# Ranks in place of due times: a new order of operations for an attention and feed-forward kernel on one core

## The chip, the cores and the metric

The kernel runs on one core of a Trainium2 chip. A core has a matrix engine (TensorE, PE in the profile; its weight loads are listed as PEld), three engines for elementwise work (VectorE or DVE, ScalarE or ACT, GpSimd or POOL) and a queue that issues DMAs (SyncE or SP). Each engine runs its own list of instructions in order and waits for the others through semaphores. SBUF is the on-chip memory, PSUM the smaller one that TensorE writes its sums to. The metric is the time of one execution on the device in microseconds (us).

## What is computed

Attention with random features, and then a feed-forward network with GELU. Shapes: batch 8, 8 heads, 576 positions, head dimension 64, 128 features; 4608 tokens of width 512, inner width 2048; everything in fp32.

```python
def phi(x):
    proj = np.einsum('bhsd,md->bhsm', x, omega)
    sq = np.sum(x * x, axis=-1, keepdims=True) / 2.0
    h = proj - sq
    h = h - np.max(h, axis=-1, keepdims=True)
    return np.exp(h) / np.sqrt(m)
q_p, k_p = (phi(q_s), phi(k_s))          # q_s, k_s: q and k times D**-0.25
kv = np.einsum('bhsm,bhsd->bhmd', k_p, v)
z = np.sum(k_p, axis=2)
num = np.einsum('bhsm,bhmd->bhsd', q_p, kv)
den = np.einsum('bhsm,bhm->bhs', q_p, z)[..., None] + 1e-06
x = num / den                            # tokens x 512
h = x @ w_in
g = 0.5 * h * (1.0 + erf(h / sqrt(2)))
out = g @ w_out
```

The term `sq` is the same for all features of a position, so it cancels in `h - max(h)`; the kernel leaves it out.

## The kernel before

**Units and blocks.** The attention is cut into 32 units: unit `u` is one batch and a pair of heads (`u.b`, `u.j`, number `u.k`). The feed-forward part is cut into 18 blocks of 256 tokens. A block can start once the units that hold its tokens are done, so units and blocks are woven into each other: block 0 after the four units of batch 0, then as many units as the next block needs, then that block, and so on.

**Plain and split units.** Units 0 to 7 are "plain" (`unit_plain`): fp32 matmuls throughout. `pair` and `shared` project q and k onto the features into PSUM, `top` takes the negative maximum per row on DVE, the exponential goes to the SBUF buffer `et`, `kv` (18 matmuls, line 797) sums over the positions, `q_trans` and `q_copy` transpose the q part, `num_plain` multiplies, and `den`, `rcp` and `div` normalise. Units 8 to 31 are "split" (`split_pre`, `exps_op`, `split_post`): the operands are cut into a high and a low half (`x_high`, `x_low`, `k_high`, `k_low`, `q_high`, `q_low`, `v_a`, `v_b`) so that the matmuls run on fp16.

A plain unit takes its exponential in one of two ways, by `u.mode`. In mode 0 (units 0 to 3) ACT reads each 128 x 128 tile from PSUM, with the negative maximum as the bias: `exp_tiles`, line 781, 18 instructions a unit in five groups of 4, 4, 2, 4 and 4 tiles. In mode 1 (units 4 to 7) DVE first subtracts the maximum while it copies a group from PSUM to `et` (`shift_tiles`, line 786, five instructions a unit), and then one instruction takes the exponential of the whole unit in SBUF (`exps`, line 790, 128 x 2304). Split units use line 790 as well.

**Weights.** `w_in` and `w_out` come as eight pieces each of 1 MB of raw 64-bit values (`w_load`, two DMAs a piece). ACT (`w_hi`, `w_lo`), DVE (`w_shift`, `w_max`) and POOL (`w_round`) turn a piece into fp32 and find its largest value. When all pieces of a matrix are in, `wchain_a` to `wchain_f` make its scale (two small steps on PE, `wchain_b` at line 643 and `wchain_d`). Then `weights_sums` prepares `w_in` for the later blocks (`a_high`, `a_low`, `a_high2`, `a_low2`, `s_sum`, `s_high`, `s_low`) and `weights_split` cuts `w_out` into fp16 halves (`w_high`, line 602, on ACT, and `w_low`, line 605, on DVE, 16 pieces each).

**Blocks.** Block 0 uses fp32 weights (`mm1`, `gelu_plain`, `mm2_plain`). Blocks 1 to 17 use seven products of half-size matrices for the first layer, in fp16 halves: `sw1`, then `comb_a` to `comb_c` on ACT and DVE, then `sw2` (line 1279 is the matmul of both), then `gelu`, `g_high`, `g_low`, and the second layer `mm2` (lines 1327 to 1329), in 8 chunks `c`. `store` copies the sums out, `store_dma` writes them.

**The order.** No engine finds its order by itself. Each step of the work is registered with `op(engine, duration, function, ...)` with what it reads (`r`), writes (`w`) and which ring of buffers it takes a new one from (`new`; for PSUM the rings `at`, `h` and `acc`). The class `Planner` then plays the whole kernel through with these durations in `run`: at every moment each engine takes, from those operations that are ready and find a buffer, the one that is most urgent, and the operation is issued at that point of the list. `order` dependencies in `put` keep each engine to that list on the chip. What "most urgent" means is the due time: `run` works it out backwards from the start times `STARTS` and `UDUE`, adds a correction by kind of operation (`OFF`, by the name and class of unit) and one by operation (`PO`), and takes off a bonus by group (`bonus`). The durations include a price for a change of the activation table on ACT (`tsw`, 1.28 us), because exp and gelu stand in different tables.

Of the kernel before, what the change touches and what calls it, by code (L numbers as in the profile page):

```python
# [41 lines left out]
OFF = dict(a_high=-13.69, a_high2=-2.55, a_low=3.92, a_low2=30.54, back=-0.66, back_c=-53.08, block_be=18.21, block_high=2.46,  # L42
        block_high_1=-26.27, block_low=1.36, block_low_1=-19.02, block_out=1.79, block_scales=-9.32, block_spread=8.72,
        bound_a=-5.8, bound_a_a=-478.94, bound_a_b=1.62, bound_a_c=6.31, bound_b=0.18, bound_b_a=-192.28, bound_b_b=-308.58,
        bound_b_c=14.95, bound_c=-4.72, bound_c_a=85.34, bound_c_b=-108.59, bound_c_c=8.05, chain_a=-1.54, chain_b=3.92,
        chain_c=66.41, chain_d=2.96, comb_a=0.61, comb_a_1=1.25, comb_b=-1.27, comb_b_1=-14.65, comb_c=-0.14, comb_c_1=-8.99,
        den_a=-450.06, den_b=-18.7, div_a=-474.39, div_b=-35.9, exp_tiles_a=88.01, exps=3.6, exps_b=74.83, exps_c=21.55,
        g_high=-0.99, g_high_1=-58.14, g_low=-11.39, g_low_1=2.86, gelu=0.98, gelu_1=3.81, gelu_plain=-27.15, identity=-18.43,
        k_high=-2.66, k_high_c=15.22, k_low=-3.41, k_low_c=-24.51, k_shift=-2.42, k_shift_c=1.96, kv_a=-4935.28, kv_a_c=86.01,
        kv_b=-28.56, kv_b2=-1.97, kv_b2_c=14.8, kv_b_c=17.09, kv_c=7.39, kv_c_c=-27.26, kv_d=2.75, kv_d_c=12.39, kv_split=-2.52,  # L50
        kv_split_c=-3.32, kvz_plain_a=-243.1, kvz_plain_b=5.35, load_dup=-31.91, load_dup_c=179.73, load_om=15.98,
        load_two_a=-43.39, load_two_b=-51.4, load_v_a=-56.35, load_v_b=-128.76, load_vst=52.48, load_vst_c=22.44, mm1=15.82,
        mm2=25.3, mm2_1=0.3, mm2_plain=18.77, norm=-13.96, norm_c=4.14, nothing=1.34, num=-6.46, num_c=15.2, num_plain_a=-13.88,
        num_plain_b=-10.89, p2=2.99, pair_a=-272.72, pair_b=121.03, proj=0.47, proj_add=0.18, proj_add_c=-12.11, proj_c=0.24,
        proj_lo=0.22, proj_lo_c=-23.83, proj_q=0.39, proj_q_c=-12.62, put_x=-2.32, put_x_c=-12.75, q_back=2.77, q_back_c=8.16,
        q_blocks=2.07, q_blocks_c=-41.78, q_copy_a=-396.58, q_copy_b=-6.38, q_high=-0.51, q_high_c=21.5, q_low=0.22,
        q_low_c=-0.57, q_max=2.12, q_max2=0.92, q_max2_c=10.36, q_max3=13.21, q_max3_c=18.46, q_max4=-11.32, q_max4_c=7.99,
        q_max5=0.92, q_max5_c=3.49, q_max6=-15.37, q_max6_c=94.79, q_max_c=-114.63, q_shift=-18.3, q_shift_c=-152.32,
        q_trans_a=513.45, q_trans_b=-13.77, rcp_a=-364.04, rcp_b=29.11, s_high=36.92, s_low=-50.32, s_sum=-467.63,
        scale_om=-24.66, shared_a=-708.55, shared_b=-11.95, shift_tiles_b=7.13, split_om=-36.34, store=-53.19, store_dma=0.58,  # L60
        sw1=0.55, sw1_1=17.68, sw2=0.57, sw2_1=2.01, t_sum=3.22, t_sum_1=-27.4, top_a=-128.4, top_b=-0.8, v_a=4.39, v_a_c=91.42,
        v_b=0.99, v_b_c=-16.74, v_max=-14.06, v_max_c=47.43, v_scales=4.0, v_spread=32.29, vb_ones=-35.4, w_abs_1=-722.49,
        w_hi_0=1.8, w_hi_1=-202.85, w_high=-23.19, w_lo_0=3.69, w_lo_1=-90.29, w_load_0=202.81, w_load_1=4.68, w_low=-134.68,
        w_max_0=5.38, w_max_1=258.53, w_round_0=-55.99, w_round_1=-43.44, w_shift_0=8.21, w_shift_1=6.84, warm=198.7,
        wchain_a=-48.44, wchain_b=43.0, wchain_c=-25.75, wchain_d=7.44, wchain_e=16.02, wchain_f=-27.17, x_high=6.09,
        x_high_c=-14.76, x_low=-3.36, x_low_c=-0.55, zeros=37.43)
# [182 lines left out]
class Planner:  # L249
# [45 lines left out]
    def run(self, lat, hop, alloc, put):  # L295
        for o in reversed(self.ops):
            k, n, x, add = o.own or (0, 0, 0.0, 0.0)
            o.due = 1e9 if k == 0 else UDUE[n] if k == 2 else add if k == 3 else add + STARTS[n] + (STARTS[n + 1] - STARTS[n] if n + 1 < len(STARTS) else 48.0) * x
            for s in o.succ:
                o.due = min(o.due, s.due - o.c - (lat.get(o.e, 0) + hop.get(s.e, 0) if s.e != o.e else 0))  # L300
# [1218 lines left out]
```

## Time and profile before

| | |
|---|---|
| median of 3 runs | 972.83 us (969.47 to 973.82) |
| the profiled execution | 974.43 us, of which the span from its first to its last instruction is 972.4 us |
| instructions | 25715 |
| mean granted TensorE clock | 0.982 |
| data moved | 71.44 MB, mean 73 GB/s |

How to read the lines below. A line of the busy times gives an engine, its busy us, its share of the span and its instructions. A row of slices has 40 digits, each the busy tenths of 1/40 of the span (24.3 us); `PEclk` is the granted clock in the same manner. A group is `line engine operation output<-inputs (shape) xcount | busy us, mean ns of one | idle us of the engine just before them <- what ended that idle time`. A wait is `waiting engine, tile and line <- what ended it: us in total, times, longest us`. The chain of work that ended last is `start us, length us, what`; it is the path that one finds by going back from the last instruction, at each step to what released it.

### The profile page before, as it was taken

To read this page: it belongs to the slowest core of one execution; us is meant where nothing else is said; L and a number is where in the kernel's file an instruction comes from. 1 tells how busy PE (TensorE), PEld (TensorE's weight loads), DVE (VectorE), ACT (ScalarE), POOL (GpSimd) and SP (SyncE) were. 2 spreads that over 40 slices of the span, in tenths; PEclk is the share of its full clock that TensorE was granted. 3 is DMA by queue.
4 is the path that set the end of the run, shared out by engine and by line. 5 is a ranking of instruction groups with operands and counts; after the bars stand their busy time and mean duration, and the time that the engine had idled before them with its cause. 6 is when DMAs were issued, how large, how long until landed. Compare 5 with 4: busy or idle time off the path is not lost.

```text
span 972.4 us, 25715 instructions
## 1 busy us (share of the span) xinstructions
PE 934.6 (96%) x9956; PEld 692.8 (71%) x9956; DVE 762.8 (78%) x2134; ACT 736.2 (76%) x1573; POOL 485.1 (50%) x717
## 2 busy tenths in 40 slices
PE   7979997889999999899999999999999999999998
PEld 6757655567776777677787777867776777786776
DVE  3878888999987998887987899788888897753432
ACT  5968868688889878877877887888787898653432
POOL 0335663775658545754638564397546764300100
PEclk7979998999999999999999999999999999999999
DMA  8865332223221313121212131212121200000000
GB/s 227 236 187 176 131 92 89 65 85 88 61 64 50 97 43 92 44 74 53 82 40 73 53 96 53 72 40 85 51 72 51 72 26 23 2 24 12 12 23 22
DMA packets 46313, 71.44 MB, mean 73 GB/s; under 512 B 13680, under 2 KB 22256, under 8 KB 46192
## 3 DMA queue, kind: packets, MB, share of 16 engines
q1 hardware_dynamic: 46192, 69.81, 23.9%
q8 instruction: 78, 1.28, 0.5%
q14 instruction: 43, 0.35, 0.1%
HBM read 60.36 MB, written 9.44 MB: 72 GB/s over the span
## 4 chain that ended last, share of the span: by engine, by line
PE 74%; DVE 9%; ACT 5%; POOL 5%; DMA 3%; issue 3%; SPq 1%; POOLq 0%; ACTq 0%; DVEq 0%
PE h L1279 26%; PE acc L1327 9%; PE acc L1328 9%; PE acc L1329 9%; PE h L1266 3%; PE acc L1320 3%; PE at L1007 2%; PE at L1092 2%; PE at L1029 2%; PE at L852 2%; PE at L797 1%; DVE w L1082 1%; DVE gl L1317 1%; DMA vt<-in_v 1%; POOL r L999 1%
## 5 line engine op out<-in xcount | busy, mean ns | idle before, releaser
L999 POOL TENSOR_TENSOR r<-xt,r 64x288 fp32r<-64x288 f32 (+2 forms) x216 | 165.9, 784 | 144.7 <-ACT r L994 83.7
L1279 PE MATMUL h<-xh,w 128*128 128x128 f16 x2176 | 216.2, 219 | 0.0
L1328 PE MATMUL acc<-woh,gl 128*128 128x512 f16 (+1 forms) x544 | 206.0, 379 | 2.5 <-DVE gl L1317 2.5
L1327 PE MATMUL acc<-woh,gh 128*128 128x512 f16 (+1 forms) x544 | 207.0, 381 | 0.9 <-ACT o L1336 0.9
L1329 PE MATMUL acc<-wol,gh 128*128 128x512 f16 (+1 forms) x544 | 205.8, 378 | 0.2 <-DVE wol L605 0.2
L1279 PE MATMUL h<-xl,w 128*128 128x128 f16 x1088 | 198.6, 219 | 0.0
L1279 PEld LDWEIGHTS <-w 128*128 128x128 f16 x3264 | 195.4, 98 | 3.3
L1279 PE MATMUL h<-xh,wih 128*128 128x128 f16 x816 | 157.2, 220 | 8.5 <-DVE gl L1317 4.8
L1279 PE MATMUL h<-xl,wih 128*128 128x128 f16 x816 | 156.5, 219 | 0.0
L1279 PE MATMUL h<-xh,wil 128*128 128x128 f16 x816 | 156.5, 219 | 0.0
L1279 PEld LDWEIGHTS <-wih 128*128 128x128 f16 x1632 | 139.7, 98 | 18.3 <-DVE h L1297 4.1
L1317 DVE SCALAR_TENSOR_TENSOR gl<-h,bs,gh 128x512 f16<-128x512 f32 x136 | 101.0, 744 | 46.2 <-ACT gh L1314 45.7
L1305 ACT ACTIVATE h<-h,bs 128x512 f32<-128x512 f32 x136 | 90.0, 662 | 49.0 <-PE h L1279 42.7
L1314 ACT ACTIVATE gh<-h,bs 128x512 f16<-128x512 f32 x136 | 93.6, 689 | 36.0 <-PE acc L1329 28.9
L1329 PEld LDWEIGHTS <-gh 128*128 128x128 f16 x560 | 55.1, 98 | 63.5 <-issue 1.7
L1279 PEld LDWEIGHTS <-wil 128*128 128x128 f16 x816 | 80.1, 98 | 17.0 <-issue 7.9
L994 ACT CAST r<-xt 128x256 fp32r<-128x256 f32 (+2 forms) x216 | 81.7, 407 | 13.2 <-PE at L1029 7.6
L1328 PEld LDWEIGHTS <-gl 128*128 128x128 f16 x560 | 55.2, 99 | 47.0 <-DVE gl L1317 3.0
L1327 PEld LDWEIGHTS <-gh 128*128 128x128 f16 x560 | 55.0, 98 | 47.2 <-issue 2.1
L1286 ACT COPY g<-h 128x256 f32<-128x256 f32 x136 | 50.4, 370 | 40.8 <-PE h L1279 38.5
L1291 DVE TENSOR_TENSOR g<-h,g 128x128 f32<-128x128 f32 x136 | 38.5, 283 | 39.0 <-ACT g L1286 38.3
L1292 DVE TENSOR_TENSOR h<-h,g 128x256 f32<-128x256 f32 x136 | 58.8, 433 | 4.7
(231 smaller groups left out, 2106.7 us busy)
## 6 DMA issues: line engine op xcount, KB each, us to landing
xt<-in_kT SPq DMA_DIRECT2D x56, 288.0 KB, 3.9
xt<-in_qT SPq DMA_DIRECT2D x56, 288.0 KB, 3.8
out_x<-o SPq DMA_DIRECT2D x35, 256.0 KB, 2.0
raw<-in_w_in SPq DMA_DIRECT2D x16, 512.0 KB, 6.6
raw<-in_w_out SPq DMA_DIRECT2D x16, 512.0 KB, 4.6
w<-in_v SPq DMA_DIRECT2D x24, 320.0 KB, 2.9
vt<-in_v SPq DMA_DIRECT2D x8, 320.0 KB, 4.6
out_x<-o SPq DMA_DIRECT2D x2, 128.0 KB, 1.8
```

The lines of the kernel that those rows point to most:

```text
L994: nc.scalar.copy(G['r', u, x][:, 0:b - a], xf[:, a:b])
L999: nc.gpsimd.tensor_tensor(r, xf[D:, a:b], r, op=ALU.subtract)
L1279: nc.tensor.matmul(h, w[p], x[r], start=first and i + m == 0, stop=last and i == 1 and m == 2, skip_group_check=True)
L1286: nc.scalar.copy(G['sa', n, c], G['h', n, c][:, 0:2 * P])
L1291: nc.vector.tensor_tensor(q, hv[:, 3], sa[:, 0:P], op=ALU.add)
L1292: nc.vector.tensor_tensor(hv[:, 1:3], hv[:, 1:3], q.unsqueeze(1).broadcast_to([P, 2, P]), op=ALU.add)
L1305: nc.scalar.activation(h, h, AF.Gelu, scale=G['bs', n][:, 2:3])
L1314: nc.scalar.activation(G['gh', n, c], G['h', n, c], AF.Copy, scale=G['bs', n][:, 3:4])
L1317: nc.vector.scalar_tensor_tensor(G['gl', n, c], G['h', n, c], G['bs', n][:, 3:4], G['gh', n, c], op0=ALU.mult, op1=ALU.subtract)
L1327: nc.tensor.matmul(acc, gh, woh[:, f, c0:c1], start=f == 0, stop=False)
L1328: nc.tensor.matmul(acc, gl, woh[:, f, c0:c1], start=False, stop=False)
L1329: nc.tensor.matmul(acc, gh, wol[:, f, c0:c1], start=False, stop=f == NF - 1)
```

## The change

Four things change at once; what each instruction computes is the same but for the second point.

1. **Ranks.** `STARTS`, `UDUE`, `OFF`, `PO`, the bonuses and the backward pass are gone. In their place stands `RANK`, a list of 4665 numbers, one for each registered operation in the order of registration. The numbers count for each engine by itself: the 1181 operations of PE have the ranks 0 to 1180, the 1384 of ACT 0 to 1383, the 1349 of DVE, 599 of POOL and 150 of SP likewise. Of the operations that are ready, the one with the lowest rank goes first.
2. **Exponentials of units 4 to 7.** `X['tiles']=8` puts these units into mode 0, so they use `exp_tiles` instead of `shift_tiles` and `exps`. The choice of PSUM rings stays as it was (by `u.b` instead of `u.mode`).
3. **Durations.** Some 20 durations that the plan assumes are set anew, and on PE 0.057 us is added where a projection of a split unit follows other kinds of work (`psw`, `ptab`).
4. **Small things.** `store` is now entered as a user of the buffer `bs` that it reads. `put` gets code for filling idle time of PE with extra matmuls, which is multiplied by `fill=0.0` and issues nothing.

```diff
-X = dict(fb=0.0, fbp=0.0, fb0=-33.65, fbb=0.17, fbw=46.38, pm=0.15, tsw=1.28, plain=8, kvp=8, eb0=8, ttr=1,
+X = dict(pm=0.15, tsw=1.28, psw=0.057, plain=8, tiles=8, fill=0.0, kvp=8, eb0=8, ttr=1,
...
-STARTS = (116.55, 138.26, 186.0, 230.93, 278.01, 329.62, 369.41, 415.44, 460.86, 506.44, 553.03, 597.34, 643.92, 691.78, 735.98,
...
+RANK = (0, 0, 0, 0, 1, 5, 2, 3, 8, 1, 2, 49, 4, 7, 2, 3, 5, 9, 16, 17, 13, 11, 3, 17, 38, 30, 4, 11, 13, 14, 2, 12, 19, 13, 20, 23, 25, 21, 23, 36,
...
+        1151, 1154, 1155, 1150, 1153, 1369, 1337, 1338, 1159, 1371, 1372, 1341, 1158, 1161, 1163, 1156, 1157, 1370, 1339, 1340, 1160, 1373, 1374,
...
+PO = {}
...
     def run(self, lat, hop, alloc, put):
-        for o in reversed(self.ops):
-            k, n, x, add = o.own or (0, 0, 0.0, 0.0)
...
-            o.due += PO.get(o.id, 0.0)
         for o in self.ops:
-            o.due += OFF.get(o.tag, 0.0)
+            o.due = RANK[o.id]
...
-                if o.tab and o.tab != self.tab:
+                if o.e == 'PE':
+                    c += X['psw'] * (o.tab == 'r' and self.ptab is None)
+                    self.ptab = o.tab
+                elif o.tab and o.tab != self.tab:
...
-                    p = (o.due - bonus.get(o.kind, 0.0), o.id)
+                    p = o.due
...
-            op('POOL', 0.84, s_sum, c, k, ...
-        op('ACT', 0.6, a_high, c, r=[a, sc], w=[('ah', c)], kind='W')
-        op('DVE', 0.75, a_low, c, r=[a, sc, ('ah', c)], w=[('al', c)], kind='W')
-        op('ACT', 0.38, a_high2, c, r=[b, sc], w=[('ah2', c)], kind='W')
-        op('DVE', 0.42, a_low2, c, r=[b, sc, ('ah2', c)], w=[('al2', c)], kind='W')
+            op('POOL', 0.78, s_sum, c, k, ...
+        op('ACT', 0.68, a_high, c, r=[a, sc], w=[('ah', c)], kind='W')
+        op('DVE', 0.92, a_low, c, r=[a, sc, ('ah', c)], w=[('al', c)], kind='W')
+        op('ACT', 0.46, a_high2, c, r=[b, sc], w=[('ah2', c)], kind='W')
+        op('DVE', 0.47, a_low2, c, r=[b, sc, ('ah2', c)], w=[('al2', c)], kind='W')
...
-            u.mode = 0 if b == 0 else 1 if u.k < X['plain'] else 2
+            u.mode = 0 if u.k < X['tiles'] else 1 if u.k < X['plain'] else 2
...
-        ring = ANY if u.mode == 0 else 'at'
-        op('PE', 1.0, num_plain, u, half, ...
-        op('ACT', 0.5, den, u, half, r=pn, new=[('dt', ('dt', u, half))])
+        ring = ANY if u.b == 0 else 'at'
+        op('PE', 1.15, num_plain, u, half, ...
+        op('ACT', 0.35, den, u, half, r=pn, new=[('dt', ('dt', u, half))])
...
-        op('PE', 0.77, kv_split, u, ...
+        op('PE', 0.87, kv_split, u, tab='q', ...
...
-                    op('ACT', 0.68 if n else 0.6, store, n, i, c0, c1, r=[key] + ([('bo', n)] if n >= N32 else []), ...
+                    op('ACT', 0.68 if n else 0.6, store, n, i, c0, c1, r=[key] + ([('bo', n), ('bs', n)] if n >= N32 else []), ...
...
     def put(o):
         n = len(nc.cur_bb.bb.instructions)
+        if X['fill'] and o.idle > 0.9 and o.t > 5.0:
...
         o.fn(*o.a)
```

The other durations that change: `x_low` 0.26 to 0.2 us plus its part by size, `norm` 0.75 to 0.85, `num` 0.47 to 0.46, `back` and `put_x` shorter by 0.02 and 0.11, `q_back` 0.74 to 0.71, `t_sum` 0.84 to 0.79, `block_high` and `block_low` longer by some 0.06 and 0.14, `comb_a` 0.37 to 0.33, `g_high` 0.7 to 0.66.

More of the change, by code (lines that the diff above doesn't have):

```diff
@@ L42 @@
[L42 to L66, printed above, removed]
@@ L295, in run @@
     def run(self, lat, hop, alloc, put):
[L296 to L303 removed]
         for o in self.ops:
[L305 removed]
+            o.due = RANK[o.id]
             o.left, o.ready, o.end, o.out = len(o.deps) + len(o.after), 0.0, None, False
         free, cand = {e: 0.0 for e in ('PE', 'ACT', 'DVE', 'POOL', 'SP')}, {e: [] for e in ('PE', 'ACT', 'DVE', 'POOL', 'SP')}
[L308 to L309 removed]
+        self.tab, self.ptab, self.dma, now, n = None, None, 0.0, 0.0, 0
         port = {'DVE': 0.0, 'POOL': 0.0}
@@ L319, in emit @@
                 alloc(name, k)
+            o.idle = t - max(free[o.e], o.free) if o.e == 'PE' else 0.0
             put(o)
@@ L349, in room @@
         def room(o):
-            t, o.pick, taken = o.ready, [], {}
+            t, o.pick, taken, o.free = o.ready, [], {}, 0.0
             if o.e == 'POOL':
@@ L373, in room @@
                 t = max(t, best[0])
+                o.free = max(o.free, best[0])
                 o.pick.append(best[1])
@@ L455, in favor_attention_ffn @@
     wi32 = w32f[:, 1].rearrange("p c (j w) -> p c j w", j=NJ)
+    id16 = ident.bitcast(BF16)
     ones = cp.tile([1, P], F32, name="ones")
@@ L921, in out_ops @@
         pn = [('pn', u, half, a) for a in range(2)]
-        ring = ANY if u.mode == 0 else 'at'
-        op('PE', 1.0, num_plain, u, half, r=[('qh', u, g) for g in (0, 1, 2)] + [('kvz', u), ('qh', u)] + old, w=keys, new=[(ring, k) for k in pn] + new)
-        op('ACT', 0.5, den, u, half, r=pn, new=[('dt', ('dt', u, half))])
+        ring = ANY if u.b == 0 else 'at'
+        op('PE', 1.15, num_plain, u, half, r=[('qh', u, g) for g in (0, 1, 2)] + [('kvz', u), ('qh', u)] + old, w=keys, new=[(ring, k) for k in pn] + new)
+        op('ACT', 0.35, den, u, half, r=pn, new=[('dt', ('dt', u, half))])
         op('DVE', 1.13, rcp, u, half, r=[('dt', u, half)], new=[('rt', ('rt', u, half)), ('rc', ('rc', u, half))])
@@ L938, in out_split @@
             keys, new, old = places(u, ps)
-            op('PE', 0.11 * n + 0.03, back, u, g, r=[('nx', u), ('nx', u, 0), ('nx', u, 1), 'ident'], new=[(('at', 'h'), ('px', u, g))])
-            op('ACT', sum(0.17 + (c1 - c0) / 1200 for _, c0, c1, _ in ps), put_x, u, g, due=(2, 2 * u.k + g, 0.0, 0.0), r=[('px', u, g)] + old, w=keys, new=new)
+            op('PE', 0.11 * n + 0.01, back, u, g, tab='q', r=[('nx', u), ('nx', u, 0), ('nx', u, 1), 'ident'], new=[(('at', 'h'), ('px', u, g))])
+            op('ACT', sum(0.06 + (c1 - c0) / 1200 for _, c0, c1, _ in ps), put_x, u, g, due=(2, 2 * u.k + g, 0.0, 0.0), r=[('px', u, g)] + old, w=keys, new=new)
     def unit_plain(u):
@@ L1207, in split_post @@
             op('POOL' if X['klp'] else 'DVE', 0.25 + 0.3 * n if X['klp'] else 0.14 + 0.15 * n, k_low, u, g, r=es, w=[('kk', g)])
-        op('PE', 0.77, kv_split, u, r=['vb'] + [('kk', g) for g in range(len(KG))], w=[], new=[('at', pk), ('kvs', ('kvs', u)), ('kvz', ('kvz', u))])
+        op('PE', 0.87, kv_split, u, tab='q', r=['vb'] + [('kk', g) for g in range(len(KG))], w=[], new=[('at', pk), ('kvs', ('kvs', u)), ('kvz', ('kvz', u))])
         op('ACT', 0.22, kv_a, u, r=[pk], w=[('kvs', u)])
@@ L1215, in split_post @@
         for g in range(2):
-            op('DVE', 0.74, q_back, u, g, r=[('eq', u.eb, y) for y in (g, g + 2)], new=[('qt', ('qt', u, g))])
+            op('DVE', 0.71, q_back, u, g, r=[('eq', u.eb, y) for y in (g, g + 2)], new=[('qt', ('qt', u, g))])
             op('ACT', 0.62, q_high, u, g, r=[('qt', u, g)] + ([('qf', u)] if g else []), w=[('qf', u, g)], new=[] if g else [('qf', ('qf', u))])
@@ L1358, in block_prep @@
         for k in range(4):
-            op('POOL', 0.84, t_sum, n, k, r=xr + [t + (0,)] * (k == 1) + [t + (1,)] * (k == 3) + [t] * (k > 0), w=[t + (k,)], new=[] if k else [('ts', t)], kind='B')
+            op('POOL', 0.79, t_sum, n, k, r=xr + [t + (0,)] * (k == 1) + [t + (1,)] * (k == 3) + [t] * (k > 0), w=[t + (k,)], new=[] if k else [('ts', t)], kind='B')
         for p in range(4):
@@ L1362, in block_prep @@
             ts = [t] + [t + (k,) for k in range(2 * p - 4, 2 * p - 2)] if p > 1 else []
-            op('ACT', 0.16 + m / 1200, block_high, n, p, r=[('bs', n)] + (ts or xr) + xt[:1] * (p > 0), w=[('xh', n, p)], new=[] if p else [('xh', ('xh', n))], kind='B')
-            op('DVE', 0.1 + m / 940, block_low, n, p, r=[('bs', n), ('xh', n), ('xh', n, p)] + (ts or xr) + xt[1:] * (p > 0), w=[('xl', n, p)],
+            op('ACT', 0.2 + m / 1150, block_high, n, p, r=[('bs', n)] + (ts or xr) + xt[:1] * (p > 0), w=[('xh', n, p)], new=[] if p else [('xh', ('xh', n))], kind='B')
+            op('DVE', 0.24 + m / 940, block_low, n, p, r=[('bs', n), ('xh', n), ('xh', n, p)] + (ts or xr) + xt[1:] * (p > 0), w=[('xl', n, p)],
                new=[] if p else [('xl', ('xl', n))], kind='B')
@@ L1381, in ffn_first @@
                new=[] if p else [('h', hk)], due=(1, n, (c + p * .28) / NS, 0.0), kind='P')
-        op('ACT', 0.16 + 256 / 1200, comb_a, n, c, r=[hk], new=[('g', ('sa', n, c))], kind='F')
+        op('ACT', 0.33, comb_a, n, c, r=[hk], new=[('g', ('sa', n, c))], kind='F')
         op('DVE', 0.65, comb_b, n, c, r=[('sa', n, c)], w=[hk], new=[('g', ('qs', n, c))], kind='F')
@@ L1386, in ffn_first @@
         op('ACT', 0.15 + 512 / 1000, gelu, n, c, r=[('bs', n)], w=[hk], tab='g', kind='F')
-        op('ACT', 0.7, g_high, n, c, r=[('bs', n), hk], new=[('gh', ('gh', n, c))], kind='F')
+        op('ACT', 0.66, g_high, n, c, r=[('bs', n), hk], new=[('gh', ('gh', n, c))], kind='F')
         op('DVE', 0.71, g_low, n, c, r=[('bs', n), hk, ('gh', n, c)], new=[('gl', ('gl', n, c))], kind='F')
@@ L1400, in ffn_second @@
                 if c == nc_ - 1:
-                    op('ACT', 0.68 if n else 0.6, store, n, i, c0, c1, r=[key] + ([('bo', n)] if n >= N32 else []), w=[('o', n, i)] if c0 else [],
+                    op('ACT', 0.68 if n else 0.6, store, n, i, c0, c1, r=[key] + ([('bo', n), ('bs', n)] if n >= N32 else []), w=[('o', n, i)] if c0 else [],
                        new=[] if c0 else [('o', ('o', n, i))], due=(1, n + 1, (lag + i * .6) / nc_, 0.0), kind='F' if n >= N32 else 'F0')
@@ L1480, in put @@
         n = len(nc.cur_bb.bb.instructions)
+        if X['fill'] and o.idle > 0.9 and o.t > 5.0:
+            t = [G[k] for (_, k), name in zip(o.new, o.pick) if name in ANY]
+            for _ in range(int((o.idle - 0.3) * X['fill'] / 0.11) if t else 0):
+                nc.tensor.matmul(t[0][:, 0:256], id16[:, 0:P], id16, start=True, stop=True)
         o.fn(*o.a)
```

21 lines of the change are left out of this document (7 added, 14 removed), and 334 rows, old and new, of tables (PO, RANK, UDUE).

## The prediction

> **What bounds the kernel now.** The page comes first: its span, its busy times, the slices with the granted clock, the shares of the chain.
>
> ```profile
> span 972.4 us, 25715 instructions
> ...
> PE 934.6 (96%) x9956; PEld 692.8 (71%) x9956; DVE 762.8 (78%) x2134; ACT 736.2 (76%) x1573; POOL 485.1 (50%) x717
> ...
> PE   7979997889999999899999999999999999999998
> ...
> PEclk7979998999999999999999999999999999999999
> ...
> PE 74%; DVE 9%; ACT 5%; POOL 5%; DMA 3%; issue 3%; SPq 1%; POOLq 0%; ACTq 0%; DVEq 0%
> ```
>
> TensorE (PE) is busy for 934.6 of 972.4 us, and the change adds no matmul and takes none away. So a better order can win only the 37.8 us in which PE is idle, and what the lower clock costs around them: both rows of slices fall below 9 in the same places, the first, third and seventh slice. The windows by stage say how much lies where (columns: length, then busy us and instructions of PE, PEld, DVE, ACT, POOL, then granted clock, DMA share, GB/s).
>
> ```profile
> 0.00:75.00 75.00, 62.27 (x498) 48.65 (x499) 49.95 (x124) 55.84 (x130) 20.02 (x19) 0.86 0.75 221
> 75.00:150.00 75.00, 75.00 (x441) 49.54 (x439) 63.14 (x120) 59.07 (x94) 46.33 (x50) 1.00 0.38 127
> 150.00:200.00 50.00, 39.97 (x361) 26.75 (x360) 46.20 (x117) 39.12 (x83) 29.68 (x55) 0.93 0.21 64
> 200.00:500.00 300.00, 291.00 (x3360) 219.67 (x3360) 261.20 (x779) 246.99 (x543) 179.59 (x267) 0.99 0.24 69
> 500.00:850.00 350.00, 347.12 (x3968) 259.27 (x3967) 295.46 (x894) 285.77 (x640) 203.91 (x321) 1.00 0.19 55
> 850.00:972.00 122.00, 119.22 (x1338) 88.90 (x1335) 46.84 (x102) 49.40 (x87) 5.60 (x8) 1.00 0.05 19
> ```
>
> PE idles for 12.7 us in the first 75, not at all in the next 75, then for 10.0 us in the 50 in which the weights of the second layer are split, 9.0 us in 200 to 500, 2.9 us in 500 to 850 and 2.8 us at the end. Three fifths of the idle time lies in the first fifth of the span. The list of PE's waits says what ends it (us in total, times, longest), and the chain shows the longest single obstacle and what a pause does to the clock.
>
> ```profile
> PE at L797 <- ACT et L790: 5.4, 1, 5.4
> PE at L797 <- DMA vt<-in_v: 4.9, 1, 4.9
> PE h L1279 <- DVE gl L1317: 4.8, 6, 1.7
> PE h L1279 <- DVE h L1297: 2.8, 5, 1.0
> PE at L1007 <- ACT qh L836: 2.6, 2, 2.1
> PE at L832 <- ACT qh L836: 2.6, 1, 2.6
> PE acc L1328 <- DVE gl L1317: 2.5, 1, 2.5
> ```
>
> ```profile
> 24.82 2.05 PE at L797 x18
> ...
> 54.89 4.22 PE at L797 x18
> ...
> 126.16 2.68 PE h L1279 x48
> ...
> 150.31 7.37 ACT woh L602 x12
> ...
> 201.01 1.03 PE at L1092 x18
> ```
>
> No wait repeats: they are single pauses of an order that is written out ahead. The 18 matmuls of a plain unit take 2.05 us, and 4.22 us behind the wait for unit 4's exponential: a pause of 5.4 us costs 2.2 us more. In 150 to 200 DVE is busy for 46.2 of 50 us and ACT converts twelve pieces of w_out in one go, 7.4 us on the chain.
>
> **The change part by part.** *Exponentials of units 4 to 7.* The groups of lines, ACT and DVE in 40 to 150 us, and the table loads of the whole span:
>
> ```profile
> L790 ACT ACTIVATE et<-et 128x2304 f32<-128x2304 f32 x4 | 8.5, 2123 | 0.1
> ...
> L786 DVE TENSOR_TENSOR et<-at,nm 128x512 f32<-128x512 f32 (+1 forms) x20 | 11.8, 628 | 0.0
> ```
>
> ```profile
> L790 ACT ACT_TABLE_LOAD x27 | 34.6, 1283 | 0.5
> ...
> L1305 ACT ACT_TABLE_LOAD x25 | 32.1, 1283 | 2.5 <-issue 2.1
> ...
> L781 ACT ACTIVATE w<-h,nm 128x128 f32<-128x128 f32 x20 | 6.1, 425 | 1.5 <-DVE nm L777 1.5
> ...
> L1311 ACT ACT_TABLE_LOAD x3 | 3.8, 1283 | 0.1
> ...
> L781 ACT ACT_TABLE_LOAD x1 | 1.3, 1283 | 0.7 <-PEq L1512 0.7
> ```
>
> ```profile
> 40.00:150.00 110.00, 104.07 (x644) 70.97 (x642) 90.55 (x185) 86.07 (x139) 60.35 (x57) 0.95 0.48 154
> ```
>
> DVE loses 20 shifts, 11.8 us. ACT loses four exponentials, 8.5 us, and gets 4 x 18 single tiles; twenty such tiles keep it busy for 6.1 us, 0.305 each, so 72 cost 22.0: 13.5 us more. The whole exponential stands in one place; the tiles come in five groups a unit with gelu_plain between them. Read in the order of their ranks, ACT's operations change between exp and gelu 62 times, against 27 + 25 + 3 + 1 = 56 loads in the trace, so I count 6 more loads of 1.283 us, 7.7 us. ACT gets 21.2 us in all. It has 23.9 us free in 40 to 150 and 10.9 in 150 to 200, 34.8 in all: hidden, but with little left in the first stretch, and if that cover goes, what is over falls on PE. Where a tile waits on ACT for its maximum from DVE, weight conversions and gelu_plain stand behind it in the queue; POOL's rounding and PE's mm2_plain wait for those. A group also holds its PSUM buffer for four tiles, 1.2 us, where the shift held it for 0.63; 20 groups make 12 us of longer holding, in 75 to 150 beside a PE that had other work throughout. I take 0 for it, and up to 12 on the bad side.
>
> The Trainium skill speaks against this part: "ScalarE: Activation LUTs", section "Table sets: the hidden batching unit", asks to do all functions of one table set before changing to the next, and its section "What ACT_TABLE_LOAD costs" puts a change at about 2.66 us, load and drain. By that figure the six loads would be an estimated 16 us instead of 7.7. The trace agrees on the load and shows only 0.5 us of idle time before 27 of them.
>
> *Order.* Each engine now takes, of what its plan finds ready, the operation with the lowest rank. In the table w_out's first scale operation on PE (wchain_b) has rank 132, ahead of the first product of block 1 (135). In the trace that product starts at 126.16 and the scale 19 us later:
>
> ```profile
> 145.22 0.27 PE L643 MATMUL at<-ident,wcm 128*1 128x128 f32 x1
> ```
>
> The operations behind the scale, sixteen conversions on ACT and sixteen on DVE, can then begin while PE still has plain units in hand, and DVE, which is full in 150 to 200, has 11.8 us less to do ahead of it. I take the 7.4 us of conversions off the path; the ends are 0 and the whole stage, 10.0 idle plus 7% of 50 us of clock, 13.5.
>
> In 0 to 75 the 5.4 us before L797 and the 2.2 us behind it can go, since unit 4's tiles start as soon as each maximum stands; behind them other products of the same unit wait for copies on ACT, so I take half, 3.8. Against it SP now issues a piece of w_in ahead of unit 0's inputs, and unit 1's values ahead of unit 0's:
>
> ```profile
> GB/s 227 236 187 176 131 92 89 65 85 88 61 64 50 97 43 92 44 74 53 82 40 73 53 96 53 72 40 85 51 72 51 72 26 23 2 24 12 12 23 22
> ...
> raw<-in_w_in SPq DMA_DIRECT2D x16, 512.0 KB, 6.6
> ...
> vt<-in_v SPq DMA_DIRECT2D x8, 320.0 KB, 4.6
> ```
>
> Two halves of 512 KB at 236 GB/s put the first product back by 4.4 us. But PE waits 4.9 us for those values anyway, and these come later only by unit 1's 320 KB, 1.4 us. So the start costs 1.4 to 4.4; I take 2.0, near the lower end, since the wait it fills is in the trace. The stage gives -1.8. POOL, the other queue that is reordered, has 28.7 of 75 us free in 75 to 150; nothing is priced for it.
>
> *Durations.* These emit nothing; they only decide how well the plan meets the chip. Rows beside old and new value:
>
> ```profile
> L620 DVE SCALAR_TENSOR_TENSOR wil<-w,wsc,wih 128x512 f16<-128x512 f32 x8 | 7.9, 1015 | 0.2 <-ACT wih L614 0.2
> ...
> L614 ACT ACTIVATE wih<-w,wsc 128x512 f16<-128x512 f32 x8 | 5.5, 713 | 0.2 <-POOL wsc L659 0.2
> ```
>
> a_low goes from 0.75 to 0.92 (1.015 measured), a_high from 0.60 to 0.68 (0.713), kv_split from 0.77 to 0.87 (1.03 for the 18 matmuls of L1092 on the chain above). Every one of these moves towards the trace, so fewer operations should arrive later than planned. In 200 to 850 this and the ranks are all there is. I take half of the idle time, 4.5 of 9.0 and 1.4 of 2.9. The ends are all of it and, the other way, as much again, since a new order can meet new pauses. store now also counts as a user of bs in the plan: nothing is issued for it, and bs has four buffers. The fill matmuls are multiplied by 0.
>
> *Sum*, against the profiled execution's 974.43 us: -1.8 - 7.4 - 4.5 - 1.4 = -15.1, so 959.3. That execution lies 1.6 above the median of 972.83; the median becomes about 958.
>
> **The rivals.** *ACT becomes the bound (slower).* Tiles wait for maxima, gelu_plain comes between, and every group may need a load before and after it: 40 loads instead of at most 8 for four whole exponentials, 32 x 1.283 = 41.1. With the 13.5 that is 54.6 us against 34.8 free, 19.8 over. With only the steady part's -5.9 kept, 974.4 + 19.8 - 5.9 = 988, 987 as a median. It decides from (34.8 - 13.5) / 1.283 = 17 added loads on. Against it speaks the rank table with its six; for it that ranks are wishes and what is ready decides. That is where the rule cited above would lead. By the 2.66 us of the Trainium skill's page "ScalarE: Activation LUTs" ("What ACT_TABLE_LOAD costs") the limit would be an estimated 8 loads.
>
> *The ranks do little.* An operation is taken only when the plan finds it ready, so the pauses move but stay as long: the idle 37.8 us remain, and the start's +2 and a few us of gain cancel. 970 to 975. For it speaks that the waits above are single ones with many causes; against it that half of the idle time sits in two stages whose work the change does move.
>
> *The pauses go nearly everywhere.* 13.5 in 150 to 200, 11.9 in 200 to 850, 7.6 less 1.4 in the front: -31.7, a median of about 941. For it speaks the stretch 75 to 150, where PE has no idle time at all; against it the start, which DMA sets.
>
> **How the numbers follow.** Forecast (950 to 968) 0.55, pauses gone (below 950) 0.12, ranks do little (968 to 978) 0.19, ACT or new pauses (above 978) 0.14. A measurement of this kernel can tell about 0.5%, 4.9 us, from no change, so faster means below 968 and slower above 977.7: 0.67, 0.19 and 0.14. The predicted time is 958. The range leaves out the far end of either rival: 943 to 979.
>
> **What would show it.** Right: PE busy for over 44 of the 50 us in 150 to 200, with the conversions L602 begun before 140; no wait of several us of PE for unit 4's exponential; L790 x24; some 60 table loads; PE's idle time in 200 to 500 nearer 5 than 9. Wrong: ACT busy above 95% in 40 to 150 with PE waiting for exp tiles, over 70 table loads, a first product of unit 0 that pushes all of the front back by 4 us, or idle time of PE in 200 to 850 of 12 us or more again.

## The result, and the profile after

The changed kernel takes 948.11 us (median of 4, 947.43 to 948.78) against 972.64 (969.47 to 973.82) before: the ratio is 0.9753, with a 95% interval of 0.9728 to 0.9777, so it is faster by 24.5 us. Its profiled execution took 947.73 us against 974.43. From here on "before" and "after" are the two kernels; the lines of the kernel's body lie 28 lower in the numbering after (L797 is L769, L790 is L762, L602 is L574, L1279 is L1251).

The page of the kernel after, first its span, busy times, slices and shares of the chain:

```profile
span 945.4 us, 25796 instructions
...
PE 924.3 (98%) x9956; PEld 687.2 (73%) x9956; DVE 747.0 (79%) x2114; ACT 746.5 (79%) x1645; POOL 492.3 (52%) x717
...
PE   7899999999999999999999999999999999999998
...
PEclk9999999999999999999999999999999999999999
...
PE 75%; DVE 8%; ACT 8%; POOL 5%; issue 2%; DMA 1%; SPq 0%; POOLq 0%; ACTq 0%; DVEq 0%
```

The third and the seventh slice, where PE and its clock fell before, are full. PE does the same 9956 matmuls in 924.3 us of busy time, not 934.6: the 10.3 us between go with the clock, whose granted mean is 0.996 here and was 0.982. The other 16.7 of the 27.0 us of span are idle time of PE (37.8 before, 21.1 now). The windows by stage, with the same columns as those of before:

```profile
0.00:75.00 75.00, 66.30 (x516) 50.55 (x516) 47.00 (x123) 64.25 (x164) 25.27 (x27) 0.95 0.79 236
75.00:150.00 75.00, 73.47 (x483) 47.83 (x482) 67.67 (x115) 70.20 (x137) 39.52 (x40) 1.00 0.33 110
150.00:200.00 50.00, 48.62 (x502) 34.90 (x501) 46.56 (x135) 44.16 (x100) 37.46 (x63) 1.00 0.28 89
200.00:500.00 300.00, 294.86 (x3419) 223.54 (x3417) 263.72 (x810) 249.75 (x562) 187.47 (x271) 1.00 0.25 71
500.00:850.00 350.00, 348.75 (x4073) 263.55 (x4070) 289.69 (x865) 282.65 (x625) 202.57 (x317) 1.00 0.18 52
```

PE's idle time by stage is now 8.7, 1.5, 1.4, 5.1 and 1.3 us (before: 12.7, 0, 10.0, 9.0, 2.9). Its waits are short, and that for unit 4's exponential (L797 before, 5.4 us) is gone:

```profile
PE at L737 <- DMA xt<-in_kT: 2.8, 1, 2.8
PE h L1251 <- DVE h L1269: 2.7, 3, 1.7
...
PE h L804 <- ACT w L753: 2.4, 2, 1.7
```

Idle time leaves out what a low clock costs, so I also keep an account of lost time. Each kind of matmul has a duration at full clock (the 18 of a plain unit 2.01 us, 24 of L1251 1.34 us, as on the chain); the sum over all matmuls that have started before a moment t, taken from t, is what is lost by then. All of the matmuls together are 908.1 us of such work in each kernel of these tables. The entries depend on the durations that one takes; only differences between kernels are read from them.

```text
lost by t (us)              t = 75    150    200    500    800
before                        27.4   30.3   45.2   63.2   71.0
after                         21.8   26.0   28.8   38.4   44.0
```

So 5.6 us of the gain came in the first 75, 10.8 between 75 and 200, 8.4 in 200 to 500 and 2.2 in 500 to 800: 27.0 in all. From 200 us on such differences hardly depend on the durations. In the front they do: with the commonest step from a matmul of the kind to the next matmul as the duration, the first two are 7.0 and 9.4; with the median step, 5.5 and 11.0.

### The profile page after: what moved, and what is told of

It is laid out like the page before. It is cut to its first block, busy times and chain, and to the rows that moved or that the text cites. A ratio compares the mean times of both kernels' runs of the same rounds, so it can differ in the third digit from the quotient of the medians.

```text
span 945.4 us, 25796 instructions
## 1 busy us (share of the span) xinstructions
PE 924.3 (98%) x9956; PEld 687.2 (73%) x9956; DVE 747.0 (79%) x2114; ACT 746.5 (79%) x1645; POOL 492.3 (52%) x717
## 4 chain that ended last, share of the span: by engine, by line
PE 75%; DVE 8%; ACT 8%; POOL 5%; issue 2%; DMA 1%; SPq 0%; POOLq 0%; ACTq 0%; DVEq 0%
PE h L1251 28%; PE acc L1299 10%; PE acc L1300 10%; PE acc L1301 10%; PE at L979 3%; PE at L1001 2%; PE h L1238 2%; PE at L1064 2%; PE at L824 2%; POOL ts L1220 2%; PE acc L1292 1%; ACT et L753 1%; DVE w L609 1%; ACT woh L574 1%; ACT w L753 1%
## 5 line engine op out<-in xcount | busy, mean ns | idle before, releaser
L971 POOL TENSOR_TENSOR r<-xt,r 64x256 fp32r<-64x256 f32 (+2 forms) x216 | 168.6, 795 | 113.9 <-ACT r L966 92.6
L1251 PE MATMUL h<-xh,w 128*128 128x128 f16 x2176 | 218.3, 220 | 0.0
L1251 PE MATMUL h<-xl,w 128*128 128x128 f16 x1088 | 199.4, 219 | 0.6 <-DVE xl L1233 0.6
L1251 PEld LDWEIGHTS <-w 128*128 128x128 f16 x3264 | 195.8, 98 | 4.9 <-issue 0.7
L1251 PE MATMUL h<-xh,wih 128*128 128x128 f16 x816 | 157.1, 220 | 5.2 <-DVE h L1269 2.7
L1251 PE MATMUL h<-xl,wih 128*128 128x128 f16 x816 | 156.3, 219 | 0.3 <-DVE xl L1233 0.3
L1251 PE MATMUL h<-xh,wil 128*128 128x128 f16 x816 | 156.3, 219 | 0.0
L1251 PEld LDWEIGHTS <-wih 128*128 128x128 f16 x1632 | 139.2, 98 | 20.1 <-DVE h L1269 4.1
L1277 ACT ACTIVATE h<-h,bs 128x512 f32<-128x512 f32 x136 | 89.9, 662 | 65.8 <-PE h L1251 63.1
L966 ACT CAST r<-xt 128x256 fp32r<-128x256 f32 (+2 forms) x216 | 84.1, 408 | 14.4 <-PE at L979 5.5
L1251 PEld LDWEIGHTS <-wil 128*128 128x128 f16 x816 | 79.9, 98 | 11.9 <-issue 2.7
```

Source lines behind the costliest of these rows:

```text
L966: nc.scalar.copy(G['r', u, x][:, 0:b - a], xf[:, a:b])
L971: nc.gpsimd.tensor_tensor(r, xf[D:, a:b], r, op=ALU.subtract)
L1251: nc.tensor.matmul(h, w[p], x[r], start=first and i + m == 0, stop=last and i == 1 and m == 2, skip_group_check=True)
L1277: nc.scalar.activation(h, h, AF.Gelu, scale=G['bs', n][:, 2:3])
```

## The experiments

Three theories stood against each other. **Places**: the gain lies in a few steps that the new order moves, namely SP's first transfers, the scale of `w_out` and the waits for whole exponentials. **Relief**: it lies in the work that goes from DVE to ACT, in whatever order. **Plan**: it lies in the durations, that is, in a plan that meets the chip. (Letters in an expectation are those of that text alone.)

### Edits that the plan answers

The first eight kernels change one thing and let the plan run again. The tiles alone, in the kernel before (the corrections by operation stay with their operations):

```diff
-            u.mode = 0 if b == 0 else 1 if u.k < X['plain'] else 2
+            u.mode = 0 if u.k < X['plain'] else 2
...
-        ring = ANY if u.mode == 0 else 'at'
+        ring = ANY if u.b == 0 else 'at'
```

> The kernel before with one part of the change: units 4 to 7 take their exponentials tile by tile from PSUM; due times, corrections and durations stay (each correction stays with its operation). Theory A, the gain is in the ranks' order: no gain, 965 to 985 us, since the due times were fitted to the old operations. Theory B, the relief of DVE by 11.8 us is what empties the stretch 150 to 200: 955 to 963 us, with TensorE idle for less than 4 us in that stretch.

Measured: 1024.37 us, a ratio of 1.0541 (1.0517 to 1.0565). With the tiles alone, under the old rules, the kernel is 51 us slower.

The other way round, the changed kernel with units 4 to 7 in the old mode, each shift ranked just behind its maximum and the whole exponential just behind the last of the tiles that it replaces:

```diff
-X = dict(pm=0.15, tsw=1.28, psw=0.057, plain=8, tiles=8, ...
+X = dict(pm=0.15, tsw=1.28, psw=0.057, plain=8, tiles=4, ...
...
```

> The changed kernel with the other part undone: units 4 to 7 shift on DVE and take one whole exponential again; a shift gets the rank just behind its maximum, the exponential the rank just behind the last of the tiles it replaces. Theory A: 947 to 956 us. Theory B: 958 us or more, the lost time between 125 and 200.

Measured: 974.04 us, 1.001 (0.9994 to 1.0026). All of the gain is gone.

The changed kernel with the durations of before:

```diff
-X = dict(pm=0.15, tsw=1.28, psw=0.057, ...
+X = dict(pm=0.15, tsw=1.28, psw=0.0, ...
-        op('DVE', 0.92, a_low, c, ...
+        op('DVE', 0.75, a_low, c, ...
...
```

> The changed kernel with the durations of the kernel before in its plan; ranks and tiles stay. Theory A: the ranks carry the order whatever the durations are, 947 to 955 us. Theory C, the better durations are what makes the plan fit the chip: 958 us or more, with TensorE idle for over 9 us in 200 to 500.

Measured: 982.32 us, 1.0108 (1.0089 to 1.0127). By itself this speaks for the plan. The fourth kernel says otherwise. It changes nothing but the 0.15 us that the plan adds to the end of the attention's operations:

```diff
-X = dict(pm=0.15, ...
+X = dict(pm=0.16, ...
```

> The changed kernel with one constant of the plan 0.01 us larger (pm, what is added to the end of an operation before others may use it: 0.16 for 0.15). It tells how much any new plan from the same ranks wanders. If ranks are an order that holds by itself: 947 to 951 us. If they were fitted to this exact plan: 953 us or more, and then differences of that size between the other runs mean nothing.

Measured: 974.69 us, 1.0034 (1.0011 to 1.0056). A hundredth of a microsecond in one price takes the whole gain away. The windows of this kernel, first 75 us and 200 to 500:

```profile
0.00:75.00 75.00, 58.96 (x451) 45.94 (x452) 45.37 (x117) 55.19 (x146) 21.41 (x20) 0.82 0.75 223
...
200.00:500.00 300.00, 289.64 (x3309) 218.07 (x3307) 260.34 (x782) 247.73 (x549) 187.35 (x273) 0.99 0.25 68
```

PE is busy for 58.96 us (66.30 after) and idles for 10.4 us in 200 to 500 (5.1 after, 9.0 before). This kernel has the tiles, the ranks, the 9956 matmuls and, but for that 0.01 us, the durations of after. What differs is the order that comes out, so the gain is in the order. And the ranks aren't a better rule of choice: they fit one plan, whose order they write down. In the five kernels with ranks whose plan runs otherwise (968 to 982 us, two of them below) they do about as well as the due times. An edit that makes the plan run otherwise can lose some 27 us for that alone, before its own effect shows. The three results above can't be read as the price of a part (under the due times of before no such small edit was run). Nor can those of the next three:

```diff
...
+    late_op, first_op = at['wchain_b', (0,)], at['mm2_plain', (0, NF - 1, 1, 0, DM)]
+    late_op.deps.add(first_op)
...
```

> The changed kernel; the first step of the scale of w_out on TensorE may only be issued behind the last product of block 0, about where it stood before. Everything else follows its rank. If the early scale is what emptied the stretch 150 to 200 (theory A1): 955 to 962 us, the conversions of w_out in one go again, and TensorE idle for over 5 us behind 140. If the stretch was emptied by something else (less work on DVE, other work held back): 946 to 951 us.

Measured: 967.88 us, 0.9961 (0.9944 to 0.9978), with PE busy for 37.73 of the 50 us in 150 to 200.

```diff
-            o.due = RANK[o.id]
+            o.due = RANKS.get(o.id, RANK[o.id])
...
+    head = [('load_two', 0, 0), ('load_om',), ('load_two', 1, 0), ('load_two', 1, 1), ('load_two', 0, 1), ('w_load', (1, 0)), ('w_load', (1, 1)), ('load_v', 0), ('load_v', 1)]
...
+            RANKS[o.id] = head.index(k)
```

> The changed kernel with the first nine DMAs of SP in the order of the kernel before (inputs of units 0 and 1 first, then two pieces of w_in, then the values). By the prediction the new start costs 2.0 us: 946 us. If the start is set by the values, which come behind the same bytes either way: 947 to 949 us. If the early piece of w_in pays: 950 us or more.

Measured: 974.58 us, 1.0029 (1.0013 to 1.0046).

The new durations in the kernel before, under its old rules:

```diff
-        op('DVE', 0.75, a_low, c, ...
+        op('DVE', 0.92, a_low, c, ...
...
```

> The kernel before with the durations of the changed kernel in its plan (without the 0.057 us on TensorE); due times and corrections stay, no tiles. Theory C, better durations make a better plan by themselves: 960 to 968 us. Theory A, the corrections of single operations were fitted to the old durations: 970 to 985 us.

Measured: 1004.43 us, 1.0324 (1.0291 to 1.0356). Here PE waits 16.5 us for POOL's half of x, as the list of its waits begins:

```profile
PE at L1029 <- POOL r L999: 16.5, 6, 7.0
```

So durations nearer to the trace didn't help these rules, which were fitted to others.

The eighth kernel lets the extra matmuls run for which the change has the code:

```diff
-X = dict(pm=0.15, tsw=1.28, psw=0.057, plain=8, tiles=8, fill=0.0, ...
+X = dict(pm=0.15, tsw=1.28, psw=0.057, plain=8, tiles=8, fill=1.0, ...
```

> The changed kernel with its own code for extra matmuls switched on (fill=1.0): where the plan foresees a pause of TensorE of over 0.9 us, matmuls on a buffer that is written over fill it. If the lower clock behind pauses costs what the profile suggests (granted clock 0.95 in the first 75 us): 944 to 947 us and a granted clock of 1.00 there. If the extra matmuls delay real work as much as they save: 947 to 951 us.

Measured: 947.02 us (946.63 to 947.64), 0.9737 (0.9712 to 0.9761). That is 1.1 us below the changed kernel, and the two intervals overlap; 38 extra matmuls ran, and the mean granted clock goes from 0.996 to 0.998, in the first 75 us from 0.95 to 0.98 and not to 1.00. It is the lowest median of all the kernels here, but not shown to be faster.

### Edits with the order kept

To ask for the price of a part, the order itself must stay. In the last four kernels the sequence in which the plan issues its operations, and the rings that it picks, are written down; the edit is made in that sequence; and it is issued without asking the plan again. No duration plays a part. Without an edit this gives the instruction lists of after and of before as they are.

**The scale of w_out late.** `first` is `wchain_b` of `w_out`, `gate` the last `mm2_plain` of block 0:

```diff
+    held = {first}
+    for o in seq_:
+        if o.deps & held:
+            held.add(o)
+    i, j = seq_.index(first), seq_.index(gate)
+    seq_ = seq_[:i] + [o for o in seq_[i:j + 1] if o not in held] + [o for o in seq_[i:j + 1] if o in held] + seq_[j + 1:]
```

> The changed kernel's order, written out and kept, with one edit: w_out's first scale step on PE (wchain_b) and all that depends on it in that stretch stand just behind the last fp32 second-layer matmuls of block 0; everything else keeps its place on each engine, and no duration plays a part. Theory A (the early scale is what filled 150 to 200 us): PE's idle time in that stretch comes back by 5 to 10 us, the time goes to 955 to 962. Theory B (the scale's place is one of many; work of other units fills the hole): 947 to 951. Theory C (the stretch was filled by the shorter queue on DVE): below 950, with PE still busy for over 47 of the 50 us.

Measured: 957.28 us (955.46 to 959.15), 0.9836 (0.9813 to 0.9859). Against the 0.9753 of after this is 0.0083 more, 8.1 us, known to some 3. Its chain, its longest wait of PE, and its window:

```profile
137.16 0.12 PE at L615
...
138.80 7.46 ACT woh L574 x12
146.26 0.48 ACT qh L808
...
146.78 2.19 PE at L814 x8
```

```profile
PE at L814 <- ACT qh L808: 8.3, 2, 7.5
```

```profile
75.00:150.00 75.00, 67.15 (x400) 42.88 (x399) 60.57 (x101) 62.13 (x123) 35.63 (x38) 0.94 0.28 93
```

The time is that of theory A. The step of the chain that stood in before (L602, 7.37 us for twelve conversions) is back with 7.46 us, and PE waits for it through `q_copy`, which stands behind the twelve in ACT's queue. It falls before 150 now, since all of the front lies earlier; in 150 to 200, where the expectation put the idle time, PE is busy for 49.39 us.

**SP's first transfers as before.** The edit sorts nine operations within their own places; each other engine keeps its list:

```diff
+    head = [('load_two', 0, 0), ('load_om',), ('load_two', 1, 0), ('load_two', 1, 1), ('load_two', 0, 1), ('w_load', (1, 0)), ('w_load', (1, 1)), ('load_v', 0), ('load_v', 1)]
+    at = [i for i, o in enumerate(seq_) if name_(o) in head]
+    for i, o in zip(at, sorted((seq_[i] for i in at), key=lambda o: head.index(name_(o)))):
+        seq_[i] = o
```

> The changed kernel's order, kept, only SP's first nine transfers in the order of before: unit 0's inputs ahead of the first piece of w_in, unit 0's values ahead of unit 1's. If the early w_in piece costs what the prediction charged (2.0 us, 1.4 to 4.4): 944 to 947, with the first product 3 to 4 us earlier and PE's idle time in 0 to 75 smaller. If the first 75 us are set by the values and the weights that must come anyway: 947 to 949. If the early piece pays, because the conversions of w_in hang on it: 950 or more, and w_in's scale later than 69.4.

Measured: 953.37 us (952.70 to 953.96), 0.9789 (0.9775 to 0.9804): 0.0036 above after, 3.5 us, known to some 3 (the medians are 5.3 apart). The chain of this kernel begins

```profile
4.47 7.90 DMA raw<-in_w_in
...
13.74 1.11 ACT raw L550
...
20.18 0.38 ACT w L753
...
20.60 4.22 PE at L769 x18
```

and that of after

```profile
2.62 4.75 DMA raw<-in_w_in
...
8.74 1.15 ACT raw L550
```

This is the third case: the early piece pays. The first conversion of `w_in` starts 5.0 us later. Its effect arrives at block 0, whose first matmul the timelines of the three kernels (least, median, longest ns; first and last start) put at 65.2 before, 56.8 after and 63.1 here:

```profile
L1266 PE MATMUL h<-xs,w x128: 379/379/483, 65.2 to 125.8; 128*128 128x256 f32 x128
```

```profile
L1238 PE MATMUL h<-xs,w x128: 378/379/484, 56.8 to 118.3; 128*128 128x256 f32 x128
```

```profile
L1238 PE MATMUL h<-xs,w x128: 379/379/483, 63.1 to 124.6; 128*128 128x256 f32 x128
```

PE's busy time hides it: the window of this kernel

```profile
0.00:75.00 75.00, 65.63 (x480) 51.78 (x481) 45.39 (x118) 58.48 (x155) 23.12 (x23) 0.86 0.75 227
```

has 0.7 us less than that of after, but the clock is 0.86 and not 0.95, and 36 matmuls fewer are done. One reservation: ACT's list is kept too, and it begins with that piece, so unit 0's exponentials wait behind a transfer that now comes late: their first tile starts at 16.20 instead of 11.24. The run can't tell this from the delay of the weights themselves, and in both kernels the chain comes to block 0 through ACT, over conversions of `w_in` and then tiles of unit 4. An order of ACT made for late pieces was not tried.

**Whole exponentials back.** In the order of after, each tile group of units 4 to 7 becomes a shift on DVE in its place, and the whole exponential stands right behind the unit's last shift. In unit 4 the sums over the positions come ahead of that point, so they are taken from values without exponential, and their wait for it is left out. The price found here can be too low by that:

```diff
+    for o in seq_:
+        if o.fn is exp_tiles and o.a[0].k >= NJ:
+            o.fn = shift_tiles
+            tiles_[o.a[0].k] = o
...
+    for o in tiles_.values():
+        o.fn = whole
```

> The changed kernel's order, kept, but units 4 to 7 go back to a shift on DVE at the place of each tile group and one whole exponential behind the unit's last shift: DVE gets 20 x 0.628 = 12.6 us, ACT loses 13.5 us and some table loads. If the tiles are hidden and not needed: 947 to 951. If the relief of DVE or the earlier start of each tile carries part of the gain: 953 to 960, with PE waiting for the whole exponential again in 40 to 150. If ACT's added work costs in truth: below 946.

Measured: 955.86 us (955.53 to 956.51), 0.9816 (0.9801 to 0.9831): 0.0063 above after, 6.1 us, known to some 3. So the tiles carry part of the gain. Rows of PE's waits up to 200 us and of the window of 150 to 200 show it:

```profile
PE h L1251 <- DVE h L1269: 3.6, 4, 1.2
PE at L804 <- ACT et L762: 3.5, 1, 3.5
```

```profile
150.00:200.00 50.00, 46.79 (x462) 32.21 (x460) 45.02 (x122) 39.22 (x83) 33.27 (x55) 1.00 0.28 87
```

PE waits 3.5 us for unit 4's exponential, through the transposes now. It waits 3.6 us for DVE's `comb_c` (L1269), against 0.7 after, and is busy for 1.8 us less in the stretch in which DVE cuts `w_out`.

**The tiles in the order of before.** The shifts of units 4 to 7 become tiles on ACT in their places, and the four whole exponentials go:

```diff
+    for o in seq_:
+        if o.fn is shift_tiles:
+            o.fn = exp_tiles
+        elif o.fn is exps and NJ <= o.a[0].k < X['plain']:
+            o.fn = lambda u: None
```

> The order of before, kept, with one edit: the shifts of units 4 to 7 become exponential tiles on ACT at the same places, and the four whole exponentials go. If the relief of DVE (12 us) is worth something by itself: 960 to 968, with PE's idle time in 150 to 200 below 7 us. If it isn't: 970 to 976. If ACT can't hide the 13.5 us and the table loads in an order that wasn't made for them: 978 to 990, with PE waiting for ACT in 40 to 150.

Measured: 981.85 us (981.53 to 986.26), 1.0093 (1.0067 to 1.0118), slower by some 9 us. PE's waits of this kernel, and its table loads:

```profile
PE at L797 <- ACT et L781: 9.1, 3, 5.5
PE at L842 <- ACT et L781: 6.1, 2, 4.4
...
PE at L765 <- ACT et L781: 2.4, 2, 1.7
```

```profile
L1305 ACT ACT_TABLE_LOAD x25 | 32.1, 1283 | 6.8 <-PE h L1279 5.6 <-issue 0.8
...
L790 ACT ACT_TABLE_LOAD x24 | 30.8, 1283 | 0.4
...
L781 ACT ACT_TABLE_LOAD x6 | 7.7, 1283 | 0.8 <-PEq L1544 0.7
...
L1311 ACT ACT_TABLE_LOAD x5 | 6.4, 1283 | 0.1
```

PE waits 17.6 us for tiles. The loads aren't why: there are 60, as many as after. The tiles stand in ACT's queue where the shifts stood in the whole order, behind work that was placed for other reasons. The tiles are worth some -6 us in one order and +9 in the other; so the relief of DVE, as a gain that holds by itself, falls.

The account of lost time for these four, and for the kernel with 0.16 us:

```text
lost by t (us)              t = 75    150    200    500    800
after                         21.8   26.0   28.8   38.4   44.0
scale late                    21.1   32.9   35.1   46.6   52.3
first transfers as before     27.1   31.5   34.1   45.1   50.8
whole exponentials            25.5   31.8   37.0   46.6   52.3
before, with tiles            29.1   40.3   54.1   70.9   78.6
plan with 0.16                33.3   37.5   45.8   64.2   72.2
```

By 200 us the first three lose 6.3, 5.3 and 8.2 us more than after, 19.8 in all; before loses 16.4 more. So the places are large enough to account for the gain up to 200 us. The three together come to some 3 us more than that gain: they overlap, and an edit to an order that was fitted as a whole may cost a little for that alone; no edit without meaning was run to measure it. None of the three gives back much of the gain behind 200: from 200 to 500 they lose 11.5, 11.0 and 9.6 us, after loses 9.6, before 18.0, the plan with 0.16 us 18.4. These 8.4 us, and the 2.2 behind 500, are then left to the order of the later units and blocks; no edit took that order apart. How much of them is due to the new durations with which that order was found stays open: each kernel that could have told it let the plan run again.

## Why the prediction was right or wrong

The direction was right and the time lay within the range, but 10 us under the forecast, at the upper edge of the third rival (pauses gone, below 950), which had a chance of 0.12. In terms of the profiled execution the sum was -15.1; it is -26.7. The promised signs are there: PE busy for 48.62 of 50 us in 150 to 200, 24 whole exponentials, 60 loads, 5.1 us of idle time in 200 to 500. The table loads, the tiles and the conversions of w_out after (groups, then one line of a timeline):

```profile
L1277 ACT ACT_TABLE_LOAD x26 | 33.4, 1283 | 4.4 <-PE h L1251 2.5 <-DVE h L1264 1.0 <-issue 0.4
...
L762 ACT ACT_TABLE_LOAD x24 | 30.8, 1283 | 0.4
L762 ACT ACTIVATE et<-et 128x2304 f32<-128x2304 f32 x13 | 27.6, 2125 | 0.1
...
L753 ACT ACTIVATE et<-at,nm 128x128 f32<-128x128 f32 x90 | 25.9, 417 | 0.4 <-DVE nm L749 0.3
...
L762 ACT ACTIVATE w<-w 128x2304 f32<-128x2304 f32 x11 | 23.4, 2125 | 0.1
...
L753 ACT ACT_TABLE_LOAD x5 | 6.4, 1283 | 0.1
...
L1283 ACT ACT_TABLE_LOAD x4 | 5.1, 1283 | 0.1
...
L550 ACT ACT_TABLE_LOAD x1 | 1.3, 1283 | 7.4 <-DMA raw<-in_w_in 7.4
```

```profile
L574 ACT ACTIVATE woh<-w,wsc x16: 706/712/797, 127.9 to 147.9; 128x512 f16<-128x512 f32 x16
```

**150 to 200, -7.4.** The mechanism was right and its price too; the term for the stage was too small. The conversions begin at 127.9 instead of 150, and to delay them costs 8.1 us, close to the 7.4 charged; they are still on the chain, but PE has other work beside them. What was missing is what the tiles are worth behind 75: the prediction named DVE's 11.8 us and gave them no price of their own, and the whole exponentials cost 4.5 us between 75 and 200 (8.2 by 200, less 3.7 by 75; 3.5 to 5.2 with the other durations). PE's longer waits for DVE's `comb_c` say that this is at least in part the relief of DVE. From 75 to 200 the gain is 10.8, within the ends of 0 and 13.5. One step of the reason was short as well. A rank ahead of the first product of block 1 couldn't have put the scale at 124.3 by itself, for it needs the last piece of `w_out`: the first product of block 1 now starts at 121.0, ahead of the scale after all. That piece is issued at 108.1 us instead of 125.6 (first and last start in these lines of before and after):

```profile
L573 SPq DMA_DIRECT2D raw<-in_w_out x16: 327/420/1269, 70.5 to 125.6; - x16
```

```profile
L545 SPq DMA_DIRECT2D raw<-in_w_out x16: 327/418/632, 59.4 to 108.1; - x16
```

**0 to 75, -1.8.** It came to -5.6. The -3.8 for unit 4's exponential fits: the whole exponential back costs 3.7 us by 75 (3.0 to 4.8 with the other durations). The step that failed is the +2.0 for SP's start order. It priced the early piece of `w_in` by what PE's first products wait for. Two lines of before's timelines, and one of after's, give first starts:

```profile
L765 PE MATMUL at<-om,xt x168: 272/272/579, 5.1 to 129.7; 64*128 64x128 f32 x168
```

```profile
L578 ACT ACTIVATE raw<-raw x16: 1114/1143/1293, 12.1 to 133.4; 128x1024 f32<-128x1024 f32 x16
```

```profile
L737 PE MATMUL at<-om,xt x192: 271/272/579, 8.7 to 144.8; 64*128 64x128 f32 x192
```

The products do start later, by 3.6 us, but the front hangs on ACT's list, whose conversions of `w_in` start at 8.7 instead of 12.1, and block 0 starts 8.4 us earlier; the old start alone puts it 6.3 us later. The term has the other sign: with ACT's list as it is, the old start costs 3.5 us by the ratios and 5.3 by the account (4.2 to 6.5). The two prices come to 9.0 us where the stage gained 5.6, so they overlap, or an edit costs something in an order that was not made for it.

**200 to 850, -5.9.** PE's idle time there fell by 5.5 us, almost as forecast, and the lost time by some 10: the clock beside the pauses wasn't counted. It was 0.98 in 200 to 300 and in 400 to 500 and is 1.00 there now, an estimated 4 us of these 200. The reason given, durations nearer to the trace, isn't shown. With the new ranks and the old durations, or the new durations alone, the gain isn't there, and 0.01 us in the plan undoes it.

**ACT's +21.2.** The six groups of tiles, of which the largest is shown above, came to 43.9 us for 144 tiles, 0.305 each; that is 22.7 more than the 21.2 of the 72 before. The whole exponentials came to 8.5 less, and four loads more, not six, to 5.1: 19.3 in all. From 40 to 150 us

```profile
40.00:150.00 110.00, 107.68 (x713) 73.63 (x712) 92.41 (x181) 103.54 (x212) 55.98 (x55) 0.98 0.44 140
```

ACT is busy for 103.54 of 110 us, or 94%, and PE waits at most 0.8 us for a tile there (1.7 us ahead of it). So it is hidden, and just so.

**The rivals.** That ACT becomes the bound is a real case, only not through the loads: with as many loads the tiles cost 9 us in the order of before, by their place in ACT's queue. The rule of the Trainium skill ("ScalarE: Activation LUTs", "Table sets: the hidden batching unit") to keep the functions of a set together didn't decide here: with 60 loads the kernel is faster than with 56. Of the 2.66 us a change that the Trainium skill gives ("ScalarE: Activation LUTs", "What ACT_TABLE_LOAD costs") the trace has 1.283, and 0.4 us of idle time before 24 loads together; the 4.4 before the other 26 are mostly waits for PE (2.5) and DVE (1.0). That the ranks do little is what the kernels with ranks show whose plan came out otherwise. The rival was wrong for this one plan and right for its neighbours. The third rival had 6.2, 13.5 and 11.9 us for the front, 150 to 200 and 200 to 850; the lost time fell by 5.6 in the front, 10.8 in 75 to 200 and 10.6 in 200 to 800, nearer to it than to the forecast's 1.8, 7.4 and 5.9. But PE still idles for 21.1 of the 37.8 us: pauses grew shorter and the clock came back, and they did not go nearly everywhere.

## What to carry to other kernels

A long order of work that a planner makes is one point, not a rule: to price a part of it, write the issue order down and edit that, and run an edit without meaning (here 0.01 us) before a difference is put down to a part. What stands first on a queue is priced by the longest chain behind it, here through ACT's list, not by the engine that waits for it first. Work moved to another engine has no price of its own; the same tiles won 6 us in an order made for them and lost 9 in one that was not.
